# Three layers on one core: the mixing weights' conversion spread over the whole second MLP round, the first batch's angles in its last two chunks, and the first mixing product from freed MLP slots

## The chip, the cores and the metric

The kernel runs on one core of a Trainium2 chip. Its time is the device time of the program on that core, in microseconds. Three runs of the kernel before took 1694.25, 1701.19 and 1694.98 us, a median of 1694.98.

## The reference

Three layers follow each other, on 8 batches of 576 tokens with 512 features. Cut to what matters:

```
# 1: attention by random features, 8 heads: phi = [exp(p), exp(-p)], p = x w_phi less its largest size
x = num / den                                   # (8, 576, 512)
# 2: MLP
xn = (x - mean) / sqrt(var + 1e-6) * g_ln
x  = x + max(xn @ w_ch1, 0) @ w_ch2             # 512 -> 2048 -> 512
# 3: mixing over tokens
theta = x @ w_theta
y = w_tok_r @ (x * cos(theta)) + w_tok_i @ (x * sin(theta))    # w_tok: 576 x 576
u = x + y
out = u + max(u @ w_ch, 0)
```

The data are float64 in the program's inputs (read as pairs of 32-bit words) and are taken to float32 on the chip. Every matrix product is made from a high and a low part of both operands, three matmuls for one (`mm3`, L74 to L76).

## The kernel before

**Two rounds of the MLP.** The hidden features are cut in six "pairs" of weights. Round 0 takes the pairs 0 to 2 over all tokens, round 1 the pairs 3 to 5 and, for the first chunks, pair 2. A chunk is 512 tokens, a round has 9 (`NQ`), and each chunk has one block for each pair: four blocks in the chunks 0 to 3 of round 1 (`LATE = 4`), three in the chunks 4 to 8. A block is `Hidden.first`, `flush_b` of the block before it, `Hidden.second`. `first` and `second` are a product by seven partial products on 128x256 tiles (the banks `pa`, `pb`, `pc`); ScalarE copies a bank out (`u`, `p`, L781) so that TensorE may use it again, ScalarE and VectorE make `hb` (L787, L788), VectorE adds in the banks (L797, L805, L812). `flush_b` multiplies `hb` by the second weights into four banks `acc`, and after a chunk's last block VectorE adds them to `xo` (L834), which goes to memory as `x2d` (L839). At a chunk's last block the next chunk's tokens are prepared by `tokens_b`: four sums on GpSimd (`c`, L667, L668, L672, L673) and their high and low parts (`a11h`, `s1h`, ... by L61 on ScalarE, L64 on VectorE).

**Weights of the mixing.** `loads_mix` is a generator of 35 steps (`LOADX`) that converts the weights of the third layer: a load `raw`, `mag` on ScalarE (L109), `bits` and `vs` in four instructions on VectorE (L110 to L112, L117), sums `tw` on GpSimd (L743 to L745), the parts `wc` (high on ScalarE, L61; low on VectorE, L64, or GpSimd, L67), and stores to `wtkd` in memory. `advance(1, ...)` runs these steps in between the blocks of round 1. Four of them convert `w_theta` into the tiles `wths`, which lie in slots of pair 2's weights that are free from chunk 4.

**Angles.** A batch's tokens are tiles of 128 rows, and the fifth is shared by two batches. `prep` loads a tile (L1032), transposes it on TensorE (L1035) and cuts it in parts `hx`; `theta` multiplies it by `wths` (12 matmuls) and makes sine and cosine times x in `zf`: ScalarE L1048, GpSimd L1049, VectorE L1050 to L1052, ScalarE L1053 to L1055, VectorE L1056.

**Mixing.** A batch is seven products (`mix`), each from one sum of the blocks of `zf` (`sums`, cut in parts `a`, L61 and L64) and one of the seven weights `t`, which `fetch` (L1026) loads from `wtkd` in the order 11, 21, t2, t1, t3, 22, t4. Their banks are `ma`, `mb`, `mc`. The pools of round 1 are closed before, and the pool `mz`, which holds `t`, `a` and `wch` (L1185), lies where they were.

The instructions of each engine stand in the order that the tile framework's scheduler gives them.

Of the kernel before, what the change touches and what calls it, by code (L numbers as in the profile page):

```python
# [47 lines left out]
def f32(ap):  # L48
    return ap.bitcast(F32)
# [3 lines left out]
def body(ctx, tc, qT, kT, va, wbd, g, w1, w2, wth, wtok, wch, out):  # L53
# [669 lines left out]
    def loads_mix():  # L723
        for c in range(KC):
            split64(p_st, wth[:, c, :], wths[c][:, 0, :], wths[c][:, 1, :])
            yield

        def part(x, n, k, *names, pool=False):
            t = p_st.tile([P, 4 * HS], F32R, name="wc", bufs=3).rearrange("p (a b c) -> p a b c", a=2, b=2)
            h, l = t[:, 0, :n], t[:, 1, :n]  # L730
            hi_act(h, x)
            (lo_pool if pool else lo_vec)(l, x, h)
            for j, at in enumerate(names):
                for nm in at:
# [150 lines left out]
    class Batch:  # L885
# [5 lines left out]
        def start(self, x4):  # L891
            self.xT = (mz if self.b % 2 else pm).tile([P, KC, S], F32, name=f"xT{self.b % 2}")
            self.zf = pm.tile([P, 4, 2, DM], F32, name="zf", bufs=2)
            o = (self.b % 2) * 64
            G.tensor_scalar(self.xT[:, :, 512:], x4[:, :, o:o + 64], 1.0, 0.0, op0=ALU.mult, op1=ALU.add)

# [12 lines left out]
        def cut(self, n, x, parts=1):  # L909
            t = mz.tile([P, 2, 4, 2 * P], F32R, name="a", bufs=3)  # L910
            m = 4 // parts
            for k in range(0, 4, m):
                hi_act(t[:, 0, k:k + m], x[:, k:k + m])
                lo_vec(t[:, 1, k:k + m], x[:, k:k + m], t[:, 0, k:k + m])
            self.a[n] = t

        def sums(self, parts=1):
            a11, a12, a21, a22 = (self.quad(d, ri) for d in range(2) for ri in range(2))
            sub = lambda o, x, y: G.tensor_tensor(o, x, y, op=ALU.subtract)  # L919
            self.cut("a11", a11, parts)  # L920
            G.tensor_tensor(a21, a21, a22, op=ALU.add)
            self.cut("a12", a12)
# [95 lines left out]
    def fetch(n=1):  # L1018
        for _ in range(n):
# [61 lines left out]
    def early(i, *a):  # L1081
        bs[0].prep(i, *a)
        bs[0].keep(i)

    xturn = [0]

    def new_x():
        if mz is not None:
            return mz.tile([P, DM], F32, name="x", bufs=3)
        xturn[0] += 1  # L1090
        return p_xb.tile([P, DM], F32, name="xs", tag=f"c{(xturn[0] - 1) % 3 + 1}")

    for r in range(2):
        done = 0
        for ch in range(NQ):
# [83 lines left out]
    sums = bs[0].sums(4)  # L1179
    next(sums)  # L1180
    for b in range(2):
        comb(b, z4)
    wchs = mz.tile([P, KC, 2, DM], F32R, name="wch")
    for c, d in enumerate(wc_d):
        SY.dma_start(out=f32(wchs[:, c]), in_=d)  # L1185
    for b in range(B):
        cur, nxt = bs[b], bs[b + 1] if b + 1 < B else None
        new = nxt and nxt.b % 2 == 0
        mix = cur.mix()
        if new:  # L1190
            x4, pre = shared_prep(nxt.b // 2)
        next(mix)
# [31 lines left out]
        if nxt:  # L1224
            next(sums)
# [93 lines left out]
```

## Time and profile before

| | before |
|---|---|
| runs, us | 1694.25, 1701.19, 1694.98 |
| median, us | 1694.98 |
| profiled execution, us | 1691.13 |
| its span, us | 1689.4 |
| TensorE (PE) busy | 1625.0 us, 96% of the span |
| VectorE (DVE) busy | 1270.5 us, 75% |
| ScalarE (ACT) busy | 876.8 us, 52% |
| GpSimd (POOL) busy | 725.2 us, 43% |

An engine's row is the time in which it executed something; TensorE's weight loads (PEld) go beside its matmuls. Line numbers such as L781 are those of the kernel before. Round 1 of the MLP lies from about 890 to 1256 us in the profiled execution, its chunks 4 to 8 from 1070.45; the boundaries of chunks used below are the times at which a chunk's `x2d` was issued.

### The profile page before, as it was taken

The page shows a single profiled execution, that of the slowest core. Times are in us where ns is not written, and L with a number is a line of the kernel's source. Part 1 is how long each engine was busy: PE and PEld are TensorE (multiplying, and loading weights), DVE is VectorE, ACT ScalarE, POOL GpSimd, SP SyncE. Part 2 cuts the span into 40 slices and gives each one's busy share as a digit, 9 for nine tenths or more (in the row PEclk, how much of TensorE's full clock was granted, in tenths as well). Part 3 has the DMA queues.
Part 4 walks back from the last instruction along what each step waited for, and adds up shares of the span by engine and source line. Part 5 has one row for each costly group of instructions (what it writes and reads, how often), then busy time and mean ns, then how long its engine had stood idle before and what let it go on. Part 6 is the DMA issues. An engine that isn't in the chain of part 4 may idle for free.

```text
span 1689.4 us, 29059 instructions
## 1 busy us (share of the span) xinstructions
PE 1625.0 (96%) x11080; PEld 1490.2 (88%) x11080; DVE 1270.5 (75%) x2271; ACT 876.8 (52%) x1709; POOL 725.2 (43%) x556
## 2 busy tenths in 40 slices
PE   8999999999999999999999999998987999999998
PEld 6777899999998898889899999987867999999998
DVE  8989888888987944787884444799756777888774
ACT  6777767677774643444443333444444444444441
POOL 7977988899871001221211111144213533344430
PEclk9999999999999999999999999999998999999999
DMA  5333433433323634454654222366718576765754
GB/s 189 102 97 117 115 99 104 117 106 111 110 77 122 214 119 162 138 200 181 235 194 164 75 75 75 114 227 218 273 66 315 190 242 234 251 229 189 249 211 176
DMA packets 120330, 273.82 MB, mean 162 GB/s; under 512 B 9088, under 2 KB 62720, under 8 KB 112768
## 3 DMA queue, kind: packets, MB, share of 16 engines
q1 hardware_dynamic: 120192, 271.98, 47.8%
q8 instruction: 87, 1.43, 0.3%
q14 instruction: 51, 0.42, 0.1%
HBM read 195.92 MB, written 73.92 MB: 160 GB/s over the span
## 4 chain that ended last, share of the span: by engine, by line
PE 78%; DVE 12%; DMA 3%; issue 3%; ACT 2%; POOL 1%; SPq 0%; DVEq 0%; ACTq 0%; POOLq 0%
PE acc L74 5%; PE acc L75 5%; PE acc L76 5%; PE ph L76 3%; PE ph L75 3%; PE ph L74 3%; PE pa L74 3%; PE pa L76 2%; PE pa L75 2%; PE mc L74 2%; PE mc L76 2%; PE mc L75 2%; PE ma L76 2%; PE ma L74 2%; PE ma L75 2%
## 5 line engine op out<-in xcount | busy, mean ns | idle before, releaser
L667 POOL TENSOR_TENSOR c<-xt 128x512 f32<-128x512 f32 x17 | 22.8, 1340 | 491.0 <-DMA xt<-xnd 367.2
L74 PE MATMUL acc<-wd,hb 128*128 128x512 f32 x432 | 171.5, 397 | 1.0 <-DVE xo L834 0.9
L75 PE MATMUL acc<-wd,hb 128*128 128x512 f32 x432 | 171.5, 397 | 0.0
L67 POOL TENSOR_TENSOR qp<-pf,qp 128x512 fp32r<-128x512 f32 (+1 forms) x120 | 147.8, 1255 | 13.5 <-ACT qp L61 12.9
L76 PE MATMUL acc<-wd,hb 128*128 128x512 f32 x432 | 152.5, 395 | 0.1
L304 DVE TENSOR_REDUCE m<-pj 128x4 f32<-128x512 f32 (+1 forms) x160 | 99.4, 625 | 38.7 <-PE pj L76 38.0
L64 DVE TENSOR_TENSOR kpl<-pf,kph 128x1024 fp32r<-128x1024 f32 (+1 forms) x67 | 101.3, 1512 | 11.1 <-ACT kph L61 10.9
L64 DVE TENSOR_TENSOR a<-zf,a 128x1024 fp32r<-128x1024 f32 (+1 forms) x59 | 94.7, 1618 | 16.0 <-ACT a L61 15.8
L306 DVE TENSOR_TENSOR ys<-pj,m 128x512 f32<-128x512 f32 (+1 forms) x160 | 99.6, 628 | 2.0 <-ACT qf L391 0.5
L316 ACT ACTIVATE pf<-ys 128x512 f32<-128x512 f32 (+1 forms) x160 | 85.3, 584 | 28.1 <-DVE ys L306 21.0
L61 ACT ACTIVATE a<-zf 128x1024 fp32r<-128x1024 f32 (+1 forms) x59 | 58.8, 1015 | 70.8 <-POOL zf L919 35.2
L74 PEld LDWEIGHTS acc<-wd,hb 128*128 128x128 f32 x432 | 82.4, 191 | 13.1 <-DVE xo L834 1.7
L75 PE MATMUL kv<-kpl,vh 128*65 128x256 f32 x300 | 86.2, 287 | 7.4 <-DVE kpl L64 7.4
L75 PEld LDWEIGHTS acc<-wd,hb 128*128 128x128 f32 x432 | 82.5, 191 | 11.2
L76 PEld LDWEIGHTS acc<-wd,hb 128*128 128x128 f32 x432 | 77.8, 190 | 12.4 <-DVE hb L788 0.8
L74 PE MATMUL kv<-kph,vh 128*65 128x256 f32 x300 | 86.9, 290 | 0.0
L74 PE MATMUL ma<-t,a 128*128 128x288 f32 x256 | 77.8, 305 | 8.6 <-ACT a L61 8.3
L76 PE MATMUL kv<-kph,vl 128*65 128x256 f32 x300 | 84.5, 282 | 0.0
L781 ACT ACTIVATE u<-pa 128x256 f32<-128x256 f32 x108 | 41.0, 380 | 79.5 <-PE pa L76 78.9
L76 PE MATMUL ma<-t,a 128*128 128x288 f32 x256 | 76.2, 300 | 1.4 <-DVE a L64 1.4
L1049 POOL TENSOR_SCALAR k<-k 128x512 f32<-128x512 f32 x31 | 26.8, 866 | 115.7 <-ACT k L1048 115.5
L75 PE MATMUL ma<-t,a 128*128 128x288 f32 x256 | 76.5, 299 | 0.0
(407 smaller groups left out, 6274.6 us busy)
## 6 DMA issues: line engine op xcount, KB each, us to landing
t<-wtkd SPq DMA_DIRECT2D x16, 1440.0 KB, 6.5
t<-wtkdt SPq DMA_DIRECT2D x16, 1440.0 KB, 7.3
t<-wtkdt SPq DMA_DIRECT2D x16, 1152.0 KB, 6.4
xt<-xnd SPq DMA_DIRECT2D x34, 512.0 KB, 4.8
raw<-in_w SPq DMA_DIRECT2D x32, 512.0 KB, 4.1
in<-in_va SPq DMA_DIRECT2D x30, 325.0 KB, 3.1
xd<-xo SPq DMA_DIRECT2D x48, 192.0 KB, 2.9
x<-xd SPq DMA_DIRECT2D x36, 256.0 KB, 3.0
```

Source lines behind the costliest of these rows:

```text
L61: A.activation(dst, src, AF.Copy)
L64: V.tensor_tensor(dst, src, f32(hi), op=ALU.subtract)
L67: G.tensor_tensor(dst, src, f32(hi), op=ALU.subtract)
L74: T.matmul(out_, lhsT=lh, rhs=rh, start=start, stop=False, **kw)
L75: T.matmul(out_, lhsT=lh, rhs=rl, start=False, stop=False, **kw)
L76: T.matmul(out_, lhsT=ll, rhs=rh, start=False, stop=stop, **kw)
L304: V.tensor_reduce(m[:, :2 * n], pv, axis=AX.X, op=ALU.max, apply_absolute_value=True)
L306: marks.append(V.tensor_tensor(ys[:, :2 * n, :], pv, m[:, :2 * n].unsqueeze(2).to_broadcast([P, 2 * n, NF]), op=ALU.subtract).ins)
L316: A.activation(kp[:, :2 * n, s, :], ys[:, :2 * n, :], AF.Exp, scale=sc)
L667: eng.tensor_tensor(s1, a21, a22, op=ALU.add)
L781: A.activation(t, ps, AF.Copy)
L1049: G.tensor_scalar(k, k, -MAGIC, 1.0, op0=ALU.add, op1=ALU.mult)
```

## The change

Three things change. **The 35 steps** of `loads_mix` ran in the blocks of the chunks 4 to 7 (35 steps over 11 blocks); now they run in the chunks 0 to 6 (over 24 blocks), and the four steps for `w_theta`, whose slots are free only from chunk 4, come last. **The angles** of the first batch's five tiles are made by `opening(i)`, called after each block of the last two chunks and ahead of the last one; before, the transposes of two and the angles of two tiles were in the last chunk's blocks and the rest behind it. **The first mixing product** has its own place: its operand `a11` in the slot of `xt`, its weights in the slot `wa3` of pair 3's pool and fetched at `opening(3)`, and its banks `ma` in those of `pa`. So it stands directly behind the last `flush_b`, ahead of the closing of the MLP's pools, with its loops turned so that the k from 0 to 2 of both halves go first. The fetches of 21 and t2 then are the first into `mz`.

```diff
     def loads_mix():
-        for c in range(KC):
-            split64(p_st, wth[:, c, :], wths[c][:, 0, :], wths[c][:, 1, :])
-            yield
-
...
+        for c in range(KC):
+            split64(p_st, wth[:, c, :], wths[c][:, 0, :], wths[c][:, 1, :])
             yield
...
-        def sums(self, parts=1):
+        def sums(self, parts=1, t=None):
             a11, a12, a21, a22 = (self.quad(d, ri) for d in range(2) for ri in range(2))
             sub = lambda o, x, y: G.tensor_tensor(o, x, y, op=ALU.subtract)
-            self.cut("a11", a11, parts)
+            self.cut("a11", a11, parts, t)
             G.tensor_tensor(a21, a21, a22, op=ALU.add)
+            yield
             self.cut("a12", a12)
...
         def product(self, bank, a, w, start, comb=None, d=0):
             x, wt = self.a[a], wts.pop(0)
+            late = self.b == 0 and a == "a11"
+            for k in range(3 if late else 0):
+                for ci in range(2):
+                    cs = slice(ci * P, (ci + 1) * P)
+                    mm3(bank[ci], x[:, 0, k, cs], x[:, 1, k, cs], wt[:, 0, k], wt[:, 1, k], k == 0, False,
+                        skip_group_check=True)
             for ci in range(2):
                 cs = slice(ci * P, (ci + 1) * P)
-                for k in range(4):
+                for k in range(3 if late else 0, 4):
...
-    def fetch(n=1):
+    def fetch(n=1, t=None):
...
+    def opening(i):
+        nonlocal x4, own, z4
+        pa = ps_a.tile([P, DM], F32, name="pa")
+        if i == 0:
+            x4 = pm.tile([P, KC, P], F32, name="x4")
+            bs[0].start(x4)
+            own = pm.tile([P, 8, DM], F32, name="zo", tag="zf", bufs=2)
+            z4 = own[:, 4:6]
+        else:
+            tile_ = (own[:, 2 * (i % 2)], own[:, 2 * (i % 2) + 1])
+            if i == 1:
+                theta(*pre4, z4, pa, tile_)
+            else:
+                bs[0].theta(i - 2, pa, tile_)
+        if i < 5:
+            pb = ps_b.tile([P, DM], F32, name="pb")
+            x, hl = own[:, 6 + i % 2], hls[i % 2]
+            if i == 0:
+                pre4.extend(prep(0, 4, pb, hl, x))
+                G.tensor_tensor(x4, f32(pre4[1]), f32(pre4[2]), op=ALU.add)
+                bs[0].first(x4)
+            else:
+                bs[0].prep(i - 1, pb, hl, x)
+                bs[0].keep(i - 1)
+        if i == 3:
+            fetch(1, in_slot("wa", 3, [2, 5, HS]))
...
             for n, m in enumerate(ms):
...
+                if r and last and n == 2:
+                    opening(5)
...
-                elif ch >= LATE:
-                    advance(1, min(1, (done - 4 * LATE) / (3 * (NQ - LATE) - 4)))
-                if r and last:
...
-                    if n == 0:
-                        x4, pre = shared_prep(0, pb, hls[0])
-                        bs[0].start(x4)
-                        own = pm.tile([P, 8, DM], F32, name="zo", tag="zf", bufs=2)
-                        early(0, pa, hls[1])
-                    elif n == 1:
-                        z4 = own[:, 2:4]
-                        theta(*pre, z4, pb, (own[:, 0], own[:, 1]))
-                        bs[0].theta(0, pa, (own[:, 4], own[:, 5]))
-                    else:
-                        early(1, pa, hls[0])
+                elif ch < NQ - 2:
+                    advance(1, min(1, done / (4 * LATE + 3 * (NQ - 2 - LATE) - 1)))
+                if r and ch >= NQ - 2:
+                    if not (last and n == 2):
+                        opening(3 * (ch - NQ + 2) + n)
...
-            if r and ch == NQ - 2:
+            if r and ch == NQ - 3:
                 advance(1, 1)
...
+    a11 = p_xb.tile([P, 2, 4, 2 * P], F32R, name="xs", tag="xt")
+    flush_b()
     s_ps.close()
     s_ps = ExitStack()
+    ps_mx = {"ma": pool("xma", 2)}
     ps_tr, ps_th = pool("xtp", 1), pool("xth", 1)
-    ps_mx = {"mc": pool("xmc", 2)}
-    bs[0].theta(1, None, (own[:, 6], own[:, 7]))
-    early(2, None, hls[1])
-    pt = ps_mx["mc"].tile([P, DM], F32, name="mc")
-    bs[0].theta(2, pt, (own[:, 0], own[:, 1]))
-    early(3, None, hls[0])
-    pt = ps_mx["mc"].tile([P, DM], F32, name="mc")
-    bs[0].theta(3, pt, (own[:, 4], own[:, 5]))
-    flush_b()
...
+    sums = bs[0].sums(4, a11)
+    next(sums)
+    mix = bs[0].mix()
+    next(mix)
     s_hb.close()
     s_xb.close()
     s_wb.close()
     s_mz, mz = opened(name="mz", bufs=1, side="right")
     fetch(2)
-    sums = bs[0].sums(4)
-    next(sums)
```

**ScalarE at a chunk's last block.** The rows are from chunk 1 of round 1, a chunk with four blocks; `u` are the copies that free a bank `pa`, `s1h` to `s3h` parts of the next chunk's tokens (L780, L786 and so on are the changed kernel's numbers of L781 and L787). Before:

```order
L787 ACTIVATE hb<-pc 128x256
L781 ACTIVATE u_12676<-pa 128x256
L61 ACTIVATE s2h<-c_12738 128x512
L61 ACTIVATE s1h<-c_12737 128x512
L781 ACTIVATE u_12690<-pa 128x256
L61 ACTIVATE s3h<-c_12739 128x512
```

The same place of the changed kernel:

```order
L786 ACTIVATE hb<-pc 128x256
L780 ACTIVATE u_12786<-pa 128x256
L61 ACTIVATE s2h<-c_12848 128x512
L61 ACTIVATE wc<-vs 128x576
L61 ACTIVATE wc<-vs 128x288
L61 ACTIVATE wc<-tw 128x576
L109 ACTIVATE mag<-raw 128x288
L61 ACTIVATE s1h<-c_12847 128x512
L780 ACTIVATE u_12800<-pa 128x256
L61 ACTIVATE s3h<-c_12849 128x512
```

Four instructions of the conversion now stand between the two copies that free `pa`; they were in later chunks.

**TensorE behind the MLP.** The rows go over the end of the MLP into the first mixing product (`ma<-t,a` before, `ma<-xs` of the change, since its operand and weights are in slots called `xs`); `mc<-xs,hx` are the angles. Before:

```order
L74 MATMUL mc<-xs,hx 128x512
L75 MATMUL mc<-xs,hx 128x512
L76 MATMUL mc<-xs,hx 128x512
L74 MATMUL ma<-t,a 128x288
L75 MATMUL ma<-t,a 128x288
```

The same place of the changed kernel:

```order
L76 MATMUL acc_15299<-wd,hb 128x512
L76 MATMUL acc_15300<-wd,hb 128x512
L74 MATMUL ma<-xs 128x288
L75 MATMUL ma<-xs 128x288
L76 MATMUL ma<-xs 128x288
```

The first mixing product moved up to the last matmuls of the MLP (some of which the scheduler puts among its own), and no angle stands in between.

**SyncE's queue in the same place.** The rows are DMA issues in order; the tiles 9237, 9238, 9239 and 9240 of `wtkd` are the weights 11, 21, t2 and t1. Before:

```order
L839 DMA x2d_113<-xo 128x1024
L839 DMA x2d_114<-xo 128x1024
L1026 DMA t<-wtkd_9237 128x2x1152
L1026 DMA t<-wtkd_9238 128x2880
L1070 DMA cf<-zo 64x512 x2
L1185 DMA wch<-wcd_115 128x1024
L1185 DMA wch<-wcd_116 128x1024
L1185 DMA wch<-wcd_117 128x1024
L1185 DMA wch<-wcd_118 128x1024
L1026 DMA t<-wtkdt_9239 128x2x1152
L1032 DMA x<-x2d_99 128x512
L1026 DMA t<-wtkdt_9240 128x2x1152
```

The same place of the changed kernel:

```order
L838 DMA x2d_114<-xo 128x1024
L838 DMA x2d_113<-xo 128x1024
L1039 DMA t<-wtkd_9238 128x2880
L1039 DMA t<-wtkdt_9239 128x2x1152
L1085 DMA cf<-zo 64x512 x2
L1207 DMA wch<-wcd_115 128x1024
L1207 DMA wch<-wcd_116 128x1024
L1207 DMA wch<-wcd_117 128x1024
L1207 DMA wch<-wcd_118 128x1024
L1047 DMA x<-x2d_99 128x512
L1039 DMA t<-wtkdt_9240 128x2x1152
```

The weight 11 left this stretch (it is fetched a chunk earlier), t2 went ahead of the four `wch`, and of the loads `x` one is left here ahead of t1.

## Rows read from the trace of the kernel before

**Rows 1.** The page: span, and busy time of the engines.
```profile
span 1689.4 us, 29059 instructions
...
PE 1625.0 (96%) x11080; PEld 1490.2 (88%) x11080; DVE 1270.5 (75%) x2271; ACT 876.8 (52%) x1709; POOL 725.2 (43%) x556
```

**Rows 2.** Busy time by window: chunks 3 to 8 (us, engines, TensorE clock, DMA).
```profile
1028.29:1070.45 42.16, 42.16 (x267) 38.10 (x266) 19.08 (x39) 13.96 (x35) 5.28 (x4) 1.00 0.24 83
1070.45:1102.06 31.61, 31.61 (x199) 28.52 (x198) 29.19 (x59) 15.95 (x38) 5.46 (x4) 1.00 0.43 141
1102.06:1140.51 38.45, 35.42 (x211) 31.21 (x210) 35.98 (x66) 17.64 (x44) 18.84 (x14) 0.96 0.72 236
1140.51:1181.90 41.39, 37.15 (x215) 32.83 (x214) 38.39 (x71) 19.14 (x46) 17.06 (x13) 0.92 0.68 215
1181.90:1214.42 32.52, 30.98 (x181) 27.21 (x180) 28.94 (x56) 15.73 (x38) 7.87 (x6) 0.95 0.81 281
1214.42:1256.67 42.25, 40.22 (x227) 34.52 (x226) 20.47 (x39) 15.27 (x32) 7.64 (x8) 1.00 0.21 75
```

**Rows 3.** Waits of TensorE, chunks 4 to 8: us in total, times, longest.
```profile
PE pa L74 <- ACT u L781: 6.9, 4, 3.5
PE pc L74 <- DVE c L805: 3.6, 4, 2.0
```

**Rows 4.** TensorE's timeline in chunk 6: start, us, instruction, [idle before <-releaser].
```profile
1158.07 0.49 PE L74 MATMUL pa<-a22h,wa 128*128 128x256 f32 x1 [3.55 <-ACT u L781]
...
1160.10 0.58 PE L74 MATMUL pc<-s4h,wa 128*128 128x256 f32 x1 [0.47 <-DVE c L805]
```

**Rows 5.** ScalarE's timeline in chunk 6, ahead of that copy.
```profile
1155.81 1.02 ACT L61 ACTIVATE wc<-vs 128x576 fp32r<-128x576 f32 x2 [5.70 <-DVE vs L117]
```

**Rows 6.** VectorE's timeline in chunk 6: one operation, early and late.
```profile
1147.44 1.37 DVE L117 SCALAR_TENSOR_TENSOR vs<-mag,bits 128x288 f32<-128x288 f32 x1
...
1155.33 0.45 DVE L117 SCALAR_TENSOR_TENSOR vs<-mag,bits 128x288 f32<-128x288 f32 x1
```

**Rows 7.** GpSimd's timeline in chunk 6: first and last of six in succession.
```profile
1145.72 1.30 POOL L667 TENSOR_TENSOR c<-xt 128x512 f32<-128x512 f32 x1 [9.12 <-DMA xt<-xnd]
...
1153.02 1.14 POOL L744 TENSOR_TENSOR tw<-vs,tw 128x288 f32<-128x288 f32 x1
```

**Rows 8.** Windows: round 0 with conversions; two of the stretch after the MLP.
```profile
660.00:880.00 220.00, 217.94 (x1356) 195.35 (x1357) 177.19 (x337) 106.98 (x257) 44.71 (x32) 1.00 0.52 183
1256.67:1264.70 8.03, 5.14 (x23) 3.39 (x21) 6.94 (x10) 4.82 (x8) 2.69 (x4) 1.00 0.79 278
1267.50:1290.00 22.50, 14.31 (x84) 13.49 (x85) 15.61 (x18) 8.62 (x14) 10.99 (x6) 0.77 1.01 360
```

**Rows 9.** ScalarE, groups of chunks 4 to 8: count | busy us, mean ns.
```profile
L109 ACT ACTIVATE mag<-raw 128x288 f32<-128x288 f32 x18 | 8.3, 462 | 11.4 <-DVE vs L117 6.7 <-issue 4.4 <-ACT s2h L61 0.3
...
L61 ACT ACTIVATE wc<-tw 128x576 fp32r<-128x576 f32 x8 | 5.4, 675 | 3.1 <-DMA wtkdt<-wc 2.4 <-DMA wtkd<-wc 0.6
...
L61 ACT ACTIVATE wc<-vs 128x576 fp32r<-128x576 f32 x5 | 3.4, 686 | 15.2 <-DVE vs L117 15.2
...
L61 ACT ACTIVATE s1h<-c 128x512 fp32r<-128x512 f32 x4 | 2.5, 623 | 0.0
...
L61 ACT ACTIVATE wc<-vs 128x288 fp32r<-128x288 f32 x5 | 2.1, 427 | 0.0
```

**Rows 10.** TensorE's timeline: chunk 8, the MLP's end, angles, mixing.
```profile
1243.75 0.39 PE L74 MATMUL pa<-s3h,wa 128*128 128x256 f32 x1 [1.97 <-ACT u L781]
...
1254.41 0.86 PE L76 MATMUL acc<-wd,hb 128*128 128x512 f32 x3
...
1262.21 0.40 PE L76 MATMUL mc<-xs,hx 128*128 128x512 f32 x1
...
1270.87 0.61 PE L74 MATMUL ma<-t,a 128*128 128x288 f32 x1 [8.26 <-ACT a L61]
...
1289.67 0.37 PE L74 MATMUL mc<-t,a 128*128 128x288 f32 x1 [2.12 <-DMA t<-wtkdt]
```

More of the change, by code (lines that the diff above doesn't have):

```diff
@@ L889, in __init__, with first, start @@
             self.a = {}
-        def start(self, x4):
-            self.xT = (mz if self.b % 2 else pm).tile([P, KC, S], F32, name=f"xT{self.b % 2}")
-            self.zf = pm.tile([P, 4, 2, DM], F32, name="zf", bufs=2)
+        def first(self, x4):
             o = (self.b % 2) * 64
             G.tensor_scalar(self.xT[:, :, 512:], x4[:, :, o:o + 64], 1.0, 0.0, op0=ALU.mult, op1=ALU.add)
+        def start(self, x4):
+            self.xT = xTs[self.b % 2]
+            self.zf = pm.tile([P, 4, 2, DM], F32, name="zf", bufs=2)
+            if self.b:
+                self.first(x4)
         def prep(self, i, *a):
@@ L907, in quad, with cut @@
             return self.zf[:, :, ri, d * 2 * P:(d + 1) * 2 * P]
-        def cut(self, n, x, parts=1):
-            t = mz.tile([P, 2, 4, 2 * P], F32R, name="a", bufs=3)
+        def cut(self, n, x, parts=1, t=None):
+            if t is None:
+                t = mz.tile([P, 2, 4, 2 * P], F32R, name="a", bufs=3)
             m = 4 // parts
@@ L915, in cut @@
             self.a[n] = t
-        def sums(self, parts=1):
+        def sums(self, parts=1, t=None):
             a11, a12, a21, a22 = (self.quad(d, ri) for d in range(2) for ri in range(2))
             sub = lambda o, x, y: G.tensor_tensor(o, x, y, op=ALU.subtract)
-            self.cut("a11", a11, parts)
+            self.cut("a11", a11, parts, t)
             G.tensor_tensor(a21, a21, a22, op=ALU.add)
+            yield
             self.cut("a12", a12)
@@ L964, in mix @@
         def mix(self):
-            self.u = [mz.tile([P, KC, S], F32R, name=f"u{i}") for i in range(2)]
             a = self.bank("ma")
-            fetch()
+            if self.b:
+                fetch()
             self.product(a, "a11", "11", True)
@@ L971, in mix @@
             yield
+            self.u = us
             b = self.bank("mb")
@@ L1024, in fetch, with prep @@
             m = 5 if w in ("21", "t3", "22", "t4") else 4
-            t = mz.tile([P, 2, 5, HS], F32R, name="t", bufs=3)
+            if t is None:
+                t = mz.tile([P, 2, 5, HS], F32R, name="t", bufs=3)
             SY.dma_start(out=f32(t[:, :, :m]), in_=wtk_d[w][:, :, :m])
             wts.append(t)
-    def prep(p, t, ps=None, hl=None):
-        x = new_x()
+            t = None
+    def prep(p, t, ps=None, hl=None, x=None):
+        if x is None:
+            x = mz.tile([P, DM], F32, name="x", bufs=3)
         gt = p * NT + t
@@ L1079, in shared @@
             comb(2 * p + b, z4)
[L1081 to L1091, printed above, removed]
+    def opening(i):
[24 more added lines that the diff above has]
+            fetch(1, in_slot("wa", 3, [2, 5, HS]))
+    x4, own, z4, pre4, xTs = None, None, None, [], None
     for r in range(2):
@@ L1130, in body @@
                         advance(0, 6 / LOADB + (done - 2 * LATE) / (3 * (NQ - LATE) - 2) * (1 - 6 / LOADB))
-                elif ch >= LATE:
-                    advance(1, min(1, (done - 4 * LATE) / (3 * (NQ - LATE) - 4)))
-                if r and last:
-                    pa = ps_a.tile([P, DM], F32, name="pa")
-                    if n < 2:
-                        pb = ps_b.tile([P, DM], F32, name="pb")
-                    if n == 0:
-                        x4, pre = shared_prep(0, pb, hls[0])
-                        bs[0].start(x4)
-                        own = pm.tile([P, 8, DM], F32, name="zo", tag="zf", bufs=2)
-                        early(0, pa, hls[1])
-                    elif n == 1:
-                        z4 = own[:, 2:4]
-                        theta(*pre, z4, pb, (own[:, 0], own[:, 1]))
-                        bs[0].theta(0, pa, (own[:, 4], own[:, 5]))
-                    else:
-                        early(1, pa, hls[0])
+                elif ch < NQ - 2:
[3 more added lines that the diff above has]
+                        opening(3 * (ch - NQ + 2) + n)
                 if r == 0 and last and n >= 1:
                     prs[3 + n] = Pair(3 + n, n - 1).back(wx_d[n - 1])
-            if r and ch == NQ - 2:
+            if r and ch == NQ - 3:
                 advance(1, 1)
@@ L1153, in body @@
                 s_xm, pm = opened(name="xm", bufs=1, side="left")
+                xTs = [pm.tile([P, KC, S], F32, name="xT0")]
                 hls = [pm.tile([P, 2, KC, P], F32R, name="hx"),
@@ L1157, in body @@
             advance(0, 1)
+    a11 = p_xb.tile([P, 2, 4, 2 * P], F32R, name="xs", tag="xt")
+    flush_b()
     s_ps.close()
     s_ps = ExitStack()
+    ps_mx = {"ma": pool("xma", 2)}
     ps_tr, ps_th = pool("xtp", 1), pool("xth", 1)
-    ps_mx = {"mc": pool("xmc", 2)}
-    bs[0].theta(1, None, (own[:, 6], own[:, 7]))
-    early(2, None, hls[1])
-    pt = ps_mx["mc"].tile([P, DM], F32, name="mc")
-    bs[0].theta(2, pt, (own[:, 0], own[:, 1]))
-    early(3, None, hls[0])
-    pt = ps_mx["mc"].tile([P, DM], F32, name="mc")
-    bs[0].theta(3, pt, (own[:, 4], own[:, 5]))
-    flush_b()
     s_ac.close()
     s_ac = ExitStack()
-    ps_mx.update((n, pool("x" + n, 2, s_ac, side="right")) for n in ("ma", "mb"))
+    ps_mx.update((n, pool("x" + n, 2, s_ac, side="right")) for n in ("mb", "mc"))
+    sums = bs[0].sums(4, a11)
+    next(sums)
+    mix = bs[0].mix()
+    next(mix)
     s_hb.close()
@@ L1178, in body @@
     fetch(2)
-    sums = bs[0].sums(4)
-    next(sums)
+    wchs = mz.tile([P, KC, 2, DM], F32R, name="wch")
+    us = [mz.tile([P, KC, S], F32R, name=f"u{i}") for i in range(2)]
+    xTs.append(mz.tile([P, KC, S], F32, name="xT1"))
     for b in range(2):
         comb(b, z4)
-    wchs = mz.tile([P, KC, 2, DM], F32R, name="wch")
+    next(sums)
     for c, d in enumerate(wc_d):
@@ L1188, in body @@
         new = nxt and nxt.b % 2 == 0
-        mix = cur.mix()
+        if b:
+            mix = cur.mix()
         if new:
             x4, pre = shared_prep(nxt.b // 2)
-        next(mix)
+        if b:
+            next(mix)
         next(sums)
@@ L1224, in body @@
         if nxt:
+            next(sums)
             next(sums)
```

## The prediction

> **What bounds the kernel.** I read the page first: TensorE is busy 1625.0 of a span of 1689.4 us, the next engine 1270.5 [rows 1]. So a gain must come out of some 64 us in which TensorE waits or out of stretches in which its clock is low. Then I cut round 1 and the stretch behind it into windows, chunk by chunk [rows 2], and looked for the stretches in which the window is longer than TensorE's busy time, or its clock below 1.00. The reader is to see three things there. Chunk 4 (31.61 us) has TensorE busy throughout, although the conversion runs in it and VectorE is 92% busy (29.19 of 31.61): a chunk of three blocks needs 31.61 us. The chunks 5, 6 and 7 have the same work and take 38.45, 41.39 and 32.52. Chunk 8 takes 42.25, but three angles are in it.
>
> The loss in these chunks by their rows [rows 2]: idle TensorE 3.03 + 4.24 + 1.54 = 8.8 us in the chunks 5 to 7, and for the granted clock (1 − 0.96) × 38.45 + 0.08 × 41.39 + 0.05 × 32.52 = 1.5 + 3.3 + 1.6 = 6.4, together **15.2 us**; chunk 8 is idle for 42.25 − 40.22 = **2.0**. The waits of TensorE say on what it waits [rows 3]: on ScalarE's copy `u` (L781), 6.9 us in four waits, and on VectorE's sum `c` (L805), 3.6 in four.
>
> The timelines of chunk 6 show the mechanism. TensorE stands 3.55 us for a `u` [rows 4]. ScalarE's queue ahead of this `u` holds two `wc`, and they waited 5.70 us for VectorE's `vs` [rows 5]. VectorE was late since its operations were slow: the same `vs` operation takes 1.37 us at 1147.44 and 0.45 at 1155.33 [rows 6]. In between GpSimd works without a gap on the next tokens and on `tw` (1145.72 to 1154.16, [rows 7]). So the loss is a meeting: tokens, `tw` and conversion at a chunk's last block, with a copy that TensorE needs queued behind. The Trainium skill ("SBUF — State Buffer", Who interferes with whom) says that a VectorE instruction with two SBUF inputs and a GpSimd instruction that reads SBUF exclude each other for whole instructions; the trace agrees (1.37 against 0.45 us).
>
> Behind the MLP, TensorE ends the last `acc` matmul at 1255.27, does the angles of two tiles to 1262.61, waits 8.26 for the operand of the first mixing product, starts it at 1270.87, and gets to the product with t1 at 1289.67 after a wait for its weights [rows 10]. From there to the end it hardly waits, so the start of this product stands for the whole stretch.
>
> **The change, part by part.** *(a) The conversion spread.* Its 35 steps go from 3.2 a block (35/11) to 1.5 (35/24). VectorE without them is busy 19.08 us in a chunk of four blocks, 4.77 a block [rows 2]. In the chunks 4 to 7 it is busy 29.19 + 35.98 + 38.39 + 28.94 = 132.5, less 12 × 4.77 = 57.2: 75.3 us of conversion. Over 25 blocks that is 3.0 a block, and a chunk of three blocks comes to 23.3 of 31.61, 74%. Round 0, with the same kind of conversion in it, has VectorE 177.19 of 220 (81%) and TensorE idle only 2.06 us, at a clock of 1.00 [rows 8]. At that rate, the chunks 0 to 6 (4 × 42.16 + 3 × 31.61 = 263 us) lose 2.06/220 × 263 = **2.5**.
>
> The rate may be too kind: the order shows that in a chunk of four blocks ScalarE now has three `wc` and one `mag` between the two copies that free `pa`, at the last block, where the tokens are made. They take 0.69 + 0.43 + 0.68 + 0.46 = 2.3 us [rows 9], and the first waits for a `vs`. My estimate: from the first copy to the end of the second, ScalarE needs these 2.3, two parts of tokens at 0.62 each, a copy at about 0.4 (under `mag`'s 0.46) and some 1.3 of wait for `vs` (from its place in VectorE's queue, behind three of its operations of 0.45), 5.2 us. TensorE has meanwhile 15 matmuls on 256 columns at about 0.12 and ten on 512 at 0.235 (three take 0.86 from first start to last end, [rows 10]): 4.1. It waits 1.1 us in each of the four chunks, **4.4**. The bounds are 0 (a `vs` that is there in time) and 7.3, the price of the worst meeting above (3.55 + 0.47 of wait [rows 4] and 3.3 of clock). I take 1.1, as the tokens and `tw` are no longer in one run of GpSimd. One lowered clock spell as in chunk 5 or 7, **1.6**, I add. The chunks 0 to 7 then lose 2.5 + 4.4 + 1.6 = 8.5 in place of 15.2: **−6.7**.
>
> *(b) The angles in the chunks 7 and 8.* TensorE does the same 60 matmuls and 20 transposes, elsewhere. What they hold up there is `pa` and `pb`, as in chunk 8 now, where one wait for `u` of 1.97 us stands [rows 10]; I take the same for the six openings together, between 0 and two such waits: **0** net. A tile's chain on the other engines is hidden behind the next block (10.5 us a block in [rows 2]).
>
> *(c) The first product and the stretch behind.* Before, from the last `acc` matmul to the product with t1: 1289.67 − 1255.27 = 34.4 us. Of them the angles of two tiles are TensorE's own work, 24 × 0.235 = 5.6 and some 0.4 for transposes, which (b) moves and does not remove: 28.4 to compare. After the change TensorE has its first product (24 matmuls) there at once, and the angles' chain, the cut of the operand and 8.26 us of wait are gone. What ends last then is t1's load: it stands in SyncE's queue behind two `x2d` (1024 KB), 21 (1440), t2 (1152), four `cf` (256 in all), four `wch` (2048) and one `x` (256), with its own 1152: 7328 KB, 7.5 MB. The stretch from 1267.50 to 1290 moved 360 GB/s with the DMA share at 1.01 [rows 8]: 20.8 us, and about 1.4 from the last matmul to the first `x2d` (1256.67 against 1255.27): 22.2. **−6.2**. Bounds: at the 278 GB/s of 1256.67 to 1264.70 [rows 8] it is 28.4, no gain; were t1 not held up by `wch`, 5280 KB give 16.4, −12. I take the 360, since the queue is full all along, as there.
>
> Sum: −6.7 + 0 − 6.2 = **−12.9**. The profiled execution took 1691.13, so 1678.2; the median of the runs is 3.85 above it, so **1682** for the runs. About 0.5% (8.5 us) is what a measurement of this kernel can tell from no change.
>
> **The rivals.** *A, the forecast:* 1682, its own range 1676 to 1687. *C, full recovery:* no meeting is left, and only 2.5 of the 15.2 and nothing of chunk 8's 2.0 remain (−14.7), and t1 comes halfway to its bound (−9): 1671. For it speaks chunk 4, which loses nothing at 92% of VectorE; against it that the order puts four conversions into ScalarE's critical place. *B, half of it does not come:* either the conversion keeps its 15.2, since GpSimd's and VectorE's instructions are as many as before and still meet, now in seven chunks instead of four, and only the −6.2 remains (1689), or the loads run at 278 GB/s and only the −6.7 remains (1688). For it speaks that the stretching lasted as long as GpSimd worked [rows 6, 7]; against it round 0, which has tokens and conversions too. The Trainium skill's page named above speaks for B: its exclusion is per instruction, so by that rule spreading moves the blocked time and does not lessen it, which gives the 1689. *D, slower:* the chunks 0 to 3, which lose nothing before (chunk 3 is at 42.16 of 42.16, [rows 2]), each get a hold-up p at their last block, by the `wc` that waits for `vs` ahead of `u`. At p = 7.3 it is 4 × 7.3 + 2.5 − 15.2 − 6.2 = +10.3, 1705. It ends slower than before from p = 4.7, and slower by over 0.5% from p = 6.9. Against it: half the steps for each block, and a meeting cost that much only in chunk 6.
>
> **How the numbers follow.** A 0.48, C 0.17, B 0.22, D 0.13. The range goes from C's low end, 1664 (both its bounds, −14.7 and −12, give 1668, and the 3.85 between the profiled execution and the median need not be there again), to 1694 (B, or D with a p of 4.5), and leaves out some 0.15, most of it D. Faster by over 0.5% (under 1686.5): A and C, 0.65; within 0.5%: B and D's mild end, 0.25; slower: 0.10.
>
> **What would show it.** In the profile after: the chunks 0 to 3 at 42.2 to 44 us, each with one wait for `u` near its last block (A), none (C), or over 5 us and a clock under 0.95 (D); the chunks 5 and 6 near 32 to 34; `vs` operations of 1 us and more still beside GpSimd's, but no wait behind them (in B they end in waits). From the last `acc` matmul to the t1 product some 22 us, ended by a wait for the DMA of t1, and no wait ahead of the first product. The forecast is wrong if the openings hold up `pa` more than once (chunks 7 and 8 over 84 us with their five angles, 2 × 31.61 + 5 × 12 × 0.235 = 77.3 and transposes), or if a wait for t2 takes the place of the one for the operand.

## The result and the profile after

The changed kernel took 1671.84 us (the median; the runs go from 1668.46 to 1674.63) against 1694.62 for the kernel before: ratio 0.9856, 95% interval 0.9825 to 0.9887, 22.8 us faster. The forecast was 1682 with a range of 1664 to 1694; the result lies where rival C stood (1671), by another sum than C's: more came from the conversion than C had, and less from the stretch behind the MLP.

The profiled execution took 1672.48 us, 18.65 less than that of before. The windows of round 1 (from the last store of round 0 to the last `x2d`; us, busy time of PE, PEld, DVE, ACT, POOL, clock, DMA) of the kernel after, chunk by chunk, and then 50 us behind it:

```profile
909.11:947.90 38.79, 38.79 (x242) 34.91 (x242) 25.89 (x53) 16.30 (x39) 10.41 (x9) 1.00 0.42 146
947.90:990.05 42.15, 42.15 (x265) 38.02 (x264) 29.19 (x57) 17.42 (x43) 11.60 (x9) 1.00 0.47 155
990.05:1032.20 42.15, 42.15 (x266) 38.06 (x265) 29.16 (x57) 17.43 (x43) 11.85 (x9) 1.00 0.47 153
1032.20:1076.42 44.22, 44.22 (x281) 40.00 (x280) 29.66 (x59) 18.26 (x45) 11.74 (x10) 1.00 0.44 146
1076.42:1105.98 29.56, 29.56 (x186) 26.66 (x185) 21.24 (x45) 12.63 (x30) 5.67 (x5) 1.00 0.59 206
1105.98:1137.58 31.60, 31.60 (x199) 28.50 (x198) 27.44 (x52) 15.76 (x37) 5.74 (x4) 1.00 0.64 225
1137.58:1169.50 31.92, 31.65 (x198) 28.16 (x197) 28.40 (x51) 15.27 (x37) 7.50 (x6) 1.00 0.38 130
1169.50:1210.45 40.95, 40.95 (x244) 36.12 (x243) 25.37 (x45) 18.63 (x41) 9.95 (x10) 1.00 0.23 79
1210.45:1248.11 37.66, 37.65 (x225) 33.20 (x225) 22.26 (x39) 16.43 (x35) 7.32 (x6) 1.00 0.25 94
1248.11:1298.11 50.00, 40.21 (x236) 36.52 (x235) 32.12 (x42) 17.78 (x26) 14.79 (x11) 0.86 0.89 316
```

Read the first two numbers of each row: the window and TensorE's busy time are the same to 0.3 us in every chunk, at a clock of 1.00. Beside the rows of before [rows 2], nothing is left of the 15.2 us lost in the chunks 5 to 7, nor of the 2.0 in chunk 8, and nothing came to the chunks 0 to 3 in exchange (42.15 and 42.15; chunk 3 takes 2.1 more and chunk 4 2.1 less, a store issued later). The chunks 7 and 8 take 78.6, with five angles in them.

The waits of TensorE in the same stretch (us in total, times, longest) stand in place of [rows 3]:

```profile
PE mb L74 <- DMA t<-wtkd: 7.7, 1, 7.7
PE tp L1050 <- DMA x<-x2d: 1.2, 1, 1.2
PE th L74 <- ACT hl L61: 0.7, 1, 0.7
PE acc L76 <- DVE hb L787: 0.3, 1, 0.3
```

The waits for `u` and `c` are gone. The new one, 7.7 us, is behind the MLP. TensorE's timeline there, after (compare [rows 10]):

```profile
1246.01 0.29 PE L74 MATMUL ma<-xs 128*128 128x288 f32 x1
...
1247.85 0.63 PE L76 MATMUL acc<-wd,hb 128*128 128x512 f32 x2
...
1257.48 0.58 PE L74 MATMUL mb<-t,a 128*128 128x288 f32 x1 [7.68 <-DMA t<-wtkd]
...
1268.80 0.66 PE L1050 MATMUL tp<-ident,x 128*128 128x128 f32 x4 [1.25 <-DMA x<-x2d]
...
1274.75 0.29 PE L74 MATMUL mc<-t,a 128*128 128x288 f32 x1
```

And the issues of SyncE's queue:

```profile
1248.11 1.81 SPq L838 DMA_DIRECT2D x2d<-xo  x2
1250.02 0.38 SPq L1039 DMA_DIRECT2D t<-wtkd  x1
...
1261.28 0.57 SPq L1039 DMA_DIRECT2D t<-wtkdt  x1
```

The first product (`ma<-xs`, from 1246.01) now stands among the MLP's last matmuls, and the second (`mb`) waits for its weights 21, whose load stands behind two `x2d` of 512 KB and was issued at 1250.02. The product with t1 (`mc`, 1274.75) waits for no load any more.

**Where the 22.8 us are.** In the profiled executions round 1 takes 339.00 in place of 351.59 us (905.08 to 1256.67 before), though 6.0 us of angles came in: 18.6 on equal work. Behind it the span is 422.4 in place of 432.7, of which 6.0 are these angles: 4.3 on equal work. (Counted from the end of the last `acc` matmul instead of the store, 1255.27 before and 1248.48 after, and with the 1.8 us of the first product that now lie ahead of that end, it is 18.7 and 4.3.) Ahead of round 1, where the change touches nothing, this execution was 4.0 us slower than that of before; the medians (22.8) differ by about that much more than the two spans (18.9).

### The profile page after: what moved, and what is told of

Its sections match the earlier page's. It is cut to its first block, busy times and chain, and to the rows that moved or that the text cites. A ratio compares the mean times of both kernels' runs of the same rounds, so it can differ in the third digit from the quotient of the medians.

```text
span 1670.5 us, 29026 instructions
## 1 busy us (share of the span) xinstructions
PE 1619.9 (97%) x11080; PEld 1488.3 (89%) x11080; DVE 1276.1 (76%) x2271; ACT 875.8 (52%) x1709; POOL 723.4 (43%) x556
## 4 chain that ended last, share of the span: by engine, by line
PE 84%; DVE 9%; DMA 3%; issue 2%; POOL 1%; ACT 1%; SPq 0%; DVEq 0%; ACTq 0%; POOLq 0%
PE acc L74 6%; PE acc L75 6%; PE acc L76 6%; PE ph L75 3%; PE ph L76 3%; PE ph L74 3%; PE pa L74 3%; PE pa L76 3%; PE pa L75 3%; PE ma L74 2%; PE ma L76 2%; PE ma L75 2%; PE mc L76 2%; PE mc L74 2%; PE mc L75 2%; PE pj L74 2%
## 5 line engine op out<-in xcount | busy, mean ns | idle before, releaser
L64 DVE TENSOR_TENSOR a<-zf,a 128x1024 fp32r<-128x1024 f32 x55 | 96.3, 1759 | 12.6 <-ACT a L61 12.3
L61 ACT ACTIVATE a<-zf 128x1024 fp32r<-128x1024 f32 x55 | 57.5, 1060 | 68.3 <-POOL zf L923 32.8
L780 ACT ACTIVATE u<-pa 128x256 f32<-128x256 f32 x108 | 41.1, 381 | 71.1 <-PE pa L76 70.2
L420 ACT ACTIVATE num<-nm 65x288 f32<-65x288 f32 x128 | 50.5, 401 | 50.3 <-PE nm L76 43.2
L74 PE MATMUL ma<-t,a 128*128 128x288 f32 x248 | 74.1, 299 | 0.5 <-DVE xT L966 0.5
L75 PE MATMUL ma<-t,a 128*128 128x288 f32 x248 | 73.1, 295 | 0.0
```

What stands on the lines that cost most here:

```text
L61: A.activation(dst, src, AF.Copy)
L64: V.tensor_tensor(dst, src, f32(hi), op=ALU.subtract)
L74: T.matmul(out_, lhsT=lh, rhs=rh, start=start, stop=False, **kw)
L75: T.matmul(out_, lhsT=lh, rhs=rl, start=False, stop=False, **kw)
L420: A.activation(self.num[:, h, o:o + 288], nm, AF.Copy)
L780: A.activation(t, ps, AF.Copy)
```

## The experiments

All ratios are against the kernel before, with a 95% interval. "Loss" of three chunks is their time less 3 x 31.61; a border is the time at which a store was issued and can lie 2 or 3 us earlier or later in another kernel, so TensorE's idle time stands beside the losses where it matters.

**The spread alone** (`spread_only`): the kernel before with

```diff
-                elif ch >= LATE:
-                    advance(1, min(1, (done - 4 * LATE) / (3 * (NQ - LATE) - 4)))
+                else:
+                    advance(1, min(1, done / (4 * LATE + 3 * (NQ - 2 - LATE) - 1)))
```

and the steps for `w_theta` at the end of `loads_mix`.

> The kernel before with the 35 conversion steps over 24 blocks of round 1 and nothing else changed. Theory M (the loss of chunks 5 to 7 is a meeting: GpSimd's tokens and tw slow VectorE just where ScalarE's queue holds a bank's copy): round 1 loses nothing, as in the changed kernel, and the time falls by the 15 us lost in chunks 5 to 7, to 1678 to 1682 (ratio 0.990 to 0.993). Theory E (part of the gain in round 1 came with the openings, which spread the angles): it falls by 8 us or less, to 1686 or more, and some waits for u remain in the chunks 5 to 7.

Measured: 1678.47 us, ratio 0.9897 (0.9869 to 0.9924). The chunks 5 to 7:

```profile
1103.51:1135.11 31.60, 31.60 (x199) 28.51 (x198) 27.53 (x52) 15.77 (x37) 5.73 (x4) 1.00 0.64 225
1135.11:1167.22 32.11, 31.89 (x200) 28.47 (x199) 27.66 (x50) 14.69 (x36) 6.06 (x4) 1.00 0.33 116
1167.22:1198.67 31.45, 31.45 (x197) 28.17 (x196) 16.91 (x34) 12.27 (x30) 6.42 (x5) 1.00 0.31 107
```

A loss of 0.3 in place of 17.5. The spread alone brings 16.5 of the 22.8 us; theory E falls. The next three runs ask which part of the dense conversion had cost them.

**No steps in a chunk's last block** (`skip_last`): the kernel before with

```diff
-                elif ch >= LATE:
-                    advance(1, min(1, (done - 4 * LATE) / (3 * (NQ - LATE) - 4)))
+                elif ch >= LATE and n < len(ms) - 1:
+                    advance(1, min(1, (2 * (ch - LATE) + n + 1) / 8))
```

> The kernel before with its steps kept out of each chunk's last block, in which the next tokens are made; the other blocks of the chunks 4 to 7 take 4.4 steps each. Theory M: little is lost in the chunks 5 to 7, under 5 us of the 15, time 1682 to 1686. Theory D (density: too many steps for a block on VectorE and ScalarE, wherever GpSimd is): 4.4 steps a block overfill VectorE more than 3.2 did, the chunks lose 20 us or more, time 1698 or above.

Measured: 1695.08 us, ratio 1.0005 (0.9991 to 1.0018). Its chunks 5 to 7:

```profile
1106.89:1146.28 39.39, 35.52 (x209) 30.96 (x208) 38.80 (x71) 18.56 (x46) 19.02 (x14) 0.96 0.73 239
1146.28:1182.38 36.10, 32.58 (x194) 29.20 (x193) 31.92 (x59) 16.39 (x40) 15.74 (x12) 0.95 0.61 201
1182.38:1216.69 34.31, 32.06 (x202) 28.64 (x201) 32.07 (x58) 16.69 (x41) 9.64 (x7) 1.00 0.85 288
```

A loss of 15.0, between what theory M (under 5) and theory D (20 or more) had. But the edit did not part what theory M says meets. GpSimd in chunk 6 of this run, its first token sum and its first `tw`:

```profile
1151.31 1.52 POOL L667 TENSOR_TENSOR c<-xt 128x512 f32<-128x512 f32 x1 [9.84 <-DVE bits L110]
...
1157.65 1.65 POOL L743 TENSOR_TENSOR tw<-vs 128x576 f32<-128x576 f32 x1
```

and TensorE behind them:

```profile
1162.88 0.39 PE L74 MATMUL pa<-a22h,wa 128*128 128x256 f32 x1 [3.52 <-ACT u L781]
```

As before, `tw` follows the four token sums without a gap ([rows 7]), and TensorE then stands 3.52 us for `u` (3.55 before, [rows 4]). The steps were called in other blocks, but their work met the tokens all the same. So this run does not speak against theory M, and as the steps were denser elsewhere it does not settle theory D either.

**Without GpSimd's share of the conversion** (`no_tw`): the sums `tw` and the low parts of their four weights are left out.

```diff
-            (lo_pool if pool else lo_vec)(l, x, h)
+            if not pool:
+                lo_vec(l, x, h)
...
-            G.tensor_tensor(tw[:, 0:2], vs[:, 1:3], vs[:, 0:2], op=ALU.subtract)
...
+            tw = vs
```

> The kernel before with the sums tw and the low parts of their weights left out on GpSimd (four of the seven mixing weights hold other numbers; the high part is stored twice, so the bytes are the same). VectorE's conversion work is the same. Theory M: VectorE's operations are no longer stretched outside the tokens, the chunks 5 to 7 lose under 8 us of the 15, time 1686 to 1690. Theory D: 15 us are lost as before, time 1692 to 1697.

**GpSimd's share on VectorE** (`tw_dve`), with everything computed:

```diff
-            G.tensor_tensor(tw[:, 0:2], vs[:, 1:3], vs[:, 0:2], op=ALU.subtract)
+            V.tensor_tensor(tw[:, 0:2], vs[:, 1:3], vs[:, 0:2], op=ALU.subtract)
...
-            part(tw[:, 0:2], 2, k, ("t1",), ("t3",), pool=True)
+            part(tw[:, 0:2], 2, k, ("t1",), ("t3",))
...
```

> The kernel before with the sums tw and the low parts of their weights on VectorE in place of GpSimd: the dense conversion of before, everything computed, and VectorE with some 11 us more work in the chunks 4 to 7. Theory G (the loss is VectorE's conversion slowed by GpSimd's share of the conversion): the work handed over costs less than the slowing, the chunks 5 to 7 lose 4 to 9 us in place of 17.5, time 1684 to 1690. Theory D (VectorE simply has too many steps for a block): with more work on VectorE they lose more than 17.5, time 1697 or above.

Measured: `no_tw` 1682.91 us, ratio 0.9937 (0.9912 to 0.9961); `tw_dve` 1684.65, ratio 0.9943 (0.9923 to 0.9963). The chunks 5 to 7 of `no_tw`:

```profile
1105.30:1138.43 33.13, 33.13 (x212) 30.00 (x210) 31.75 (x70) 18.23 (x45) 5.59 (x4) 1.00 0.83 271
1138.43:1171.56 33.13, 31.95 (x201) 28.57 (x200) 29.98 (x64) 17.36 (x43) 6.30 (x4) 1.00 0.83 278
1171.56:1203.92 32.36, 31.34 (x194) 27.51 (x193) 29.71 (x59) 16.53 (x40) 6.54 (x5) 1.00 0.79 275
```

and of `tw_dve`:

```profile
1104.40:1139.47 35.07, 34.84 (x220) 31.18 (x219) 33.73 (x75) 17.30 (x44) 5.81 (x5) 1.00 0.73 239
1139.47:1169.66 30.19, 29.31 (x179) 25.90 (x178) 29.13 (x64) 15.77 (x38) 5.48 (x4) 1.00 0.77 266
1169.66:1203.33 33.67, 33.65 (x211) 29.74 (x210) 32.92 (x68) 18.88 (x44) 8.41 (x5) 1.00 0.88 302
```

Losses of 3.8 and 4.1 in place of 17.5, at the same density of steps; TensorE is idle for 2.2 and 1.1 us there, at a clock of 1.00, against 8.8 before. In `tw_dve` VectorE has more instructions and is busy for less: 95.8 us against 103.3 in [rows 2]. Part of this is a step that slid into chunk 8; over the chunks 4 to 8 it is 148.9 us for 309 instructions against 153.0 for 288. So most of the loss was VectorE's work slowed by GpSimd's part of the same conversion, and not the number of VectorE's steps in a block; theory D, which had 15 us lost in `no_tw` and over 17.5 in `tw_dve`, falls for before's density. The tokens on GpSimd, which both runs keep, cost at most the 4 us that are left. Whether `tw` costs as much where it does not follow the tokens directly, these two runs do not show, as they take `tw` off GpSimd altogether.

**Dense, but early or late** (`dense_early`, `dense_late`): the changed kernel with

```diff
-                    advance(1, min(1, done / (4 * LATE + 3 * (NQ - 2 - LATE) - 1)))
+                    advance(1, min(31 / LOADX, done / 11) if ch < LATE else min(1, (31 + 2 * (done - 4 * LATE)) / LOADX))
```

> The changed kernel with the first 31 steps at 3.2 a block, as before, but in the chunks 0 to 2 of round 1 (four blocks each, mixing of their place in the round aside), and the four steps of the angles' weights in chunk 4. Theories M and D: the density and the meetings of before are back, 8 to 15 us are lost in chunks 0 to 2, time 1680 to 1687. Rival L (the loss belongs to the late place, where the transfers fill up to 0.8 of the DMA engines): nothing is lost, 1670 to 1674.

and with

```diff
-                elif ch < NQ - 2:
-                    advance(1, min(1, done / (4 * LATE + 3 * (NQ - 2 - LATE) - 1)))
+                elif LATE <= ch < NQ - 2:
+                    advance(1, min(1, (done - 4 * LATE) / (3 * (NQ - 2 - LATE) - 1)))
```

> The changed kernel with its 35 steps in the chunks 4 to 6 alone, 3.9 a block in place of 1.5: the openings and the first product without the spread. Theories G and D: the chunks 4 to 6 lose 15 to 20 us, as the chunks 5 to 7 did before, and the time is 1685 to 1692; the part of the change that is not the spread is then worth what is left of the gain, 4 to 9 us. If under 8 us are lost there, the spread was not what brought the most.

Measured: `dense_early` 1678.21 us, ratio 0.9896 (0.9871 to 0.9921), `dense_late` 1703.83, ratio 1.0052 (1.0036 to 1.0068). The chunks 0 and 1 of `dense_early`:

```profile
907.00:951.34 44.34, 43.48 (x271) 38.63 (x271) 37.77 (x76) 20.21 (x50) 15.31 (x13) 1.00 0.54 180
951.34:995.27 43.93, 39.33 (x233) 33.89 (x233) 40.00 (x74) 19.84 (x49) 20.22 (x15) 1.00 0.72 239
```

They lose 7.3 beside the kernel after (38.79 and 42.15). The time lies between what rival L (1670 to 1674) and the other theories (1680 to 1687) had. A loss came with the density, so rival L falls as it was put, that nothing is lost here; but it is less than half of that in the late place, so the place or something that goes with it has a part. One such thing shows in GpSimd's timeline: in chunk 0 of this run it stands idle between the tokens and the next `tw`,

```profile
917.03 1.49 POOL L739 TENSOR_TENSOR tw<-vs 128x576 f32<-128x576 f32 x1 [5.37 <-DVE vs L117]
```

and TensorE's longest wait in the chunks 0 and 1 is 1.5 us, against 3.55 before, where there is no gap. This speaks for theory M's meeting, but no run changes that gap alone. The chunks 4 to 8 of `dense_late`:

```profile
1074.41:1111.34 36.93, 35.27 (x220) 31.07 (x219) 34.01 (x65) 16.83 (x41) 13.88 (x11) 1.00 0.58 191
1111.34:1149.80 38.46, 33.85 (x182) 28.37 (x181) 37.76 (x70) 17.57 (x43) 18.53 (x14) 0.91 0.76 245
1149.80:1185.70 35.90, 33.31 (x202) 28.63 (x201) 35.69 (x66) 19.88 (x46) 10.24 (x8) 1.00 0.94 320
1185.70:1235.22 49.52, 40.47 (x210) 34.49 (x209) 34.77 (x59) 21.12 (x43) 10.54 (x9) 0.90 0.26 98
1235.22:1278.34 43.12, 41.37 (x244) 35.91 (x243) 27.39 (x45) 18.98 (x41) 12.10 (x9) 1.00 0.25 89
```

16.5 lost in three chunks, as expected, and 14.0 more in the chunks 7 and 8 (92.64 against 78.61), which no theory had, so that the time missed the forecast of 1685 to 1692: the conversion's tail runs into the openings. VectorE's last conversions are still there until 1208, and TensorE waits 3.1 us for a `u` at 1199 and 4.9 for the load of an opening's tile at 1211. With a conversion this dense (3.9 steps a block, 3.2 before) the openings and the first product together leave the kernel slower than before.

**The stretch behind the MLP.** Four kernels on one chip: the changed one again (`after_again`); without the early first product (`no_first`); with the loads of 21 and t2 ahead of the last `x2d` (`early_t`); and with `wch` behind t1 as well (`early_t_wch`). The core of `no_first`:

```diff
-        if i == 3:
-            fetch(1, in_slot("wa", 3, [2, 5, HS]))
...
-    sums = bs[0].sums(4, a11)
-    next(sums)
-    mix = bs[0].mix()
-    next(mix)
...
     fetch(2)
+    sums = bs[0].sums(4)
+    next(sums)
```

and of the two others, the last hunk in `early_t_wch` alone (where the two lines stood before, they are taken out):

```diff
-                    SY.dma_start(out=x2_d[2 * ch + i], in_=x[:, i * CT:(i + 1) * CT, :])
+                    (A if ch == NQ - 1 else SY).dma_start(out=x2_d[2 * ch + i], in_=x[:, i * CT:(i + 1) * CT, :])
...
-    fetch(2)
     wchs = mz.tile([P, KC, 2, DM], F32R, name="wch")
     us = [mz.tile([P, KC, S], F32R, name=f"u{i}") for i in range(2)]
     xTs.append(mz.tile([P, KC, S], F32, name="xT1"))
+    fetch(2)
...
+        if not b:
+            for c, d in enumerate(wc_d):
+                SY.dma_start(out=f32(wchs[:, c]), in_=d)
```

> The changed kernel once more, to stand beside the three others of this set: 1669 to 1675.

> The changed kernel without its early first product: operand, weights 11 and banks are made behind the MLP, as before; the openings and the spread stay. Theory Q (the stretch behind the MLP is set by the queue of loads): the 1152 KB of weight 11 go back into it, and t1 stands behind them, 3.3 us at 360 GB/s, and TensorE gets its first product only when they have landed; 3 to 8 us over the changed kernel, 1675 to 1680. Rival P (TensorE's own 24 matmuls, 3.2 us, were what the early product took out of the way, and they fit into the wait for the loads): under 1 us, 1671 to 1673.

> The changed kernel with the tiles of the mixing pool in another order, so that the places of the weights 21 and t2 come free with the last token operands, and with the last two x2d stores issued from ScalarE's queue, so that the two loads need not stand behind them. Theory Q: the loads start some 6 us earlier, the wait of 7.68 us for 21 falls to under 4 (the operand a12 is then the later one), and the time falls by 4 to 6 us, to 1666 to 1668. Rival R (the operands' chain of sums on GpSimd and cuts sets the stretch, and the wait is only handed on): under 2 us.

> The same as early_t, and the four wch loads (2048 KB) behind the load of t1. Theory Q: t1 lands 5 us earlier, and of this the kernel gains 1 to 3 us more than early_t. Rival R: no more than early_t.

| | median, us | ratio (95%) |
|---|---|---|
| `after_again` | 1669.78 | 0.9844 (0.9828 to 0.9861) |
| `no_first` | 1676.72 | 0.9882 (0.9868 to 0.9896) |
| `early_t` | 1665.18 | 0.9814 (0.9800 to 0.9828) |
| `early_t_wch` | 1663.14 | 0.9810 (0.9792 to 0.9827) |

TensorE's waits behind the MLP in `no_first`:

```profile
1253.89 0.58 PE L74 MATMUL ma<-t,a 128*128 128x288 f32 x1 [8.62 <-DMA t<-wtkd]
...
1268.08 0.61 PE L74 MATMUL ma<-t,a 128*128 128x288 f32 x1 [4.27 <-DMA t<-wtkdt]
```

The operand is there in time (before it was the wait of 8.26, [rows 10]), but the load of the weights takes the place of that wait, 8.62, and a second load costs 4.27. The early product is worth 6.9 us, and rival P falls. In `early_t_wch` the load of 21 and the same place read:

```profile
1236.21 0.32 SPq L1039 DMA_DIRECT2D t<-wtkd  x1
```

```profile
1248.98 0.40 PE L74 MATMUL mb<-t,a 128*128 128x288 f32 x1 [1.29 <-ACT a L61]
```

The load of 21 is issued at 1236.21 and its wait is gone; the operand is late next, by 1.29 us. `early_t` has the same 1.29 us there, with the load issued at 1234.36. It gains 4.6 us over the changed kernel, as theory Q had it (4 to 6; rival R: under 2), and its slowest run (1665.99) is faster than the fastest of `after_again` (1668.66). The earlier place of the loads and the stores on ScalarE's queue came in together; which of them was needed, no run tells. That `wch` behind t1 adds 2.0 us more is within the spread of the runs and not settled. `early_t_wch` has the lowest median of all kernels run.

## Why the prediction was half right

**The reading of before held, with one part open.** TensorE's losses were in the chunks 5 to 7 and came by `u` and `c` behind slowed VectorE work. That `tw` and the low parts on GpSimd are needed for most of it is shown (`no_tw`, `tw_dve`). That they must meet the tokens in one run of GpSimd, as the prediction has it, is not shown: `skip_last` left that run as it was, and the spread both thins the steps and parts the two. In chunk 2, after, `tw` comes 10.3 us behind the tokens:

```profile
1009.21 1.43 POOL L739 TENSOR_TENSOR tw<-vs 128x576 f32<-128x576 f32 x1 [10.30 <-DVE vs L117]
```

**(a) The spread was put at −6.7; alone it measured −16.5.** The direction was right, the terms that I left standing were too large: 4.4 for four hold-ups, 1.6 for a lowered clock, 2.5 by round 0's rate. Together they are 8.5 of the 9.8 us that are missing; by their length the chunks 5 to 7 had also lost 17.5 and not the 15.2 of my sum. That the time still lies in the range is owed to the range's width. The step that failed is TensorE's cover in the hold-up. ScalarE at the last block of chunk 2, after, is as I had worked it out (5.4 us from the first copy to the second's end, `vs` waited for 1.62; estimated were 5.2 and 1.3):

```profile
1017.86 0.39 ACT L780 ACTIVATE u<-pa 128x256 f32<-128x256 f32 x1 [0.59 <-PE pa L76]
...
1020.38 1.02 ACT L61 ACTIVATE wc<-vs 128x576 fp32r<-128x576 f32 x2 [1.62 <-DVE vs L117]
...
1022.89 0.39 ACT L780 ACTIVATE u<-pa 128x256 f32<-128x256 f32 x1
```

But TensorE's rows in the same stretch show that it had work for all of it:

```profile
1017.48 0.28 PE L76 MATMUL pa<-s2h,wa 128*128 128x256 f32 x1
...
1022.51 0.28 PE L76 MATMUL pa<-s3h,wa 128*128 128x256 f32 x1
...
1025.29 0.28 PE L74 MATMUL pa<-a22h,wa 128*128 128x256 f32 x1
```

From the bank's last matmul of s2 to the first that needs the second copy (`a22`) it runs 7.8 us without a gap, where I had counted 4.1: the scheduler puts the next block's first products and more `acc` matmuls in between. The copy at 1022.89 starts 0.1 us after its own matmuls end (1022.51 + 0.28). So the price of each hold-up was 0, and D, which rested on it, did not come. The round-0 rate was no floor either: TensorE waits 0.3 us in all in the chunks 0 to 6, at a clock of 1.00.

**Rival B's rule and what it lacked.** VectorE's work for the conversion is 71.7 us after (191.0 in the chunks 0 to 6, less 25 x 4.77), against the 75.3 of before. Counted the same way, `no_tw` needs 63.4 (120.6 in the chunks 4 to 7, less 57.2); if that is taken as the price without GpSimd's share, an estimate, what came on top of it fell from 11.9 to 8.3 us only. The operation that was slowed most says the same:

```profile
L111 DVE SCALAR_TENSOR_TENSOR bits<-raw,bits 128x288 int32<-128x288 int32 x18 | 12.2, 676 | 0.6
```

This operation with two inputs took 0.68 us on average after, 0.75 before and 0.45 in `tw_dve`. So most of the slowing moved and did not go away, as B had it. The Trainium skill ("SBUF — State Buffer", Who interferes with whom) says that such a VectorE instruction and a GpSimd instruction that reads SBUF exclude each other for whole instructions; the trace agrees (0.75 us beside the dense `tw`, 0.45 without it). But B's conclusion, 1689, does not follow: with half the steps in each block the slowed work fits under TensorE's. In the chunks 5 and 6 VectorE is busy 27.4 and 28.4 us (the prediction had 23.3, an average over all blocks), and TensorE waits 0.3 us for it in all.

**(b) The openings at 0: right within what the runs tell.** `no_first`, which is spread and openings, has 0.9882 beside 0.9897 for the spread alone, with intervals that overlap. In the changed kernel the chunks 7 and 8 take 78.6 us with no wait in them; the sign of being wrong was 84. Where the conversion had not ended ahead of them the openings were not hidden (`dense_late`).

**(c) The stretch behind at −6.2: near in size, wrong in the load that ends it.** The profiled executions give 4.3, and `no_first` gives 6.9 for the first product. I had t1's load last; it was that of 21, behind the `x2d` (7.7 us). A wait for 21 took the place of the wait for the operand, which is close to the sign of being wrong that I had given (a wait for t2 there). t1 had time because TensorE did the next tile's angles first (1268.80 to 1274.75), and 26.3 us, not 22, lie between the last `acc` matmul and t1's product.

## What to carry to other kernels

Background work on two engines that slow each other (here VectorE and GpSimd) can be cheaper thin and long than dense and short, even where its total time hardly falls: ask how much of it one block of the foreground can cover. Count the cover of a late copy by the instructions that really stand in the engine's order up to the first one that needs it, not by the helper's source. Where a transition is set by loads, look at what is queued ahead of the first one (stores of the stage before), and whether its place is free earlier.

## What the runs showed of the hardware

Work handed from GpSimd to VectorE made VectorE less busy (148.9 us against 153.0 over the chunks 4 to 8, with 21 more instructions). Behind the 7.68 us wait the matmuls of 288 columns come every 0.24 us until 1263, against 0.13 before it, at a granted clock of 0.50, the lower of its two levels (1.2 of 2.4 GHz):

```profile
1257.40:1263.00 5.60, 5.52 (x23) 5.55 (x24) 0.00 (x0) 0.24 (x1) 0.87 (x1) 0.50 1.03 325
```

So the stretch pays for the wait a second time: 24 matmuls at 0.11 us more each are 2.6 us, an estimate from these rows.
